# One core: a cached attention block beside an MLP at decode, with x's rows issued by SyncE between wq's two blocks and the last but one piece of w2b in three parts

## The chip, the core and the metric

The kernel runs on one core of a Trainium2 chip. The metric is the device time of one execution in microseconds; the figure given is the median of several runs. A core has five engines that run their own instruction streams and meet at semaphores: TensorE (PE, matmuls), VectorE (DVE), ScalarE (ACT), GpSimd (POOL) and SyncE (SP). DMA transfers are issued from an engine's stream, go into a queue, and are carried by the core's 16 DMA engines.

## The reference

For two tokens (B = 2, one position each) of width 1024 it computes, in fp32:

```python
xn = layernorm(x)
q = (xn @ wq).reshape(2, 1, 32, 128)            # 32 query heads, 4 key/value heads
scores = q · k_cache * 128 ** -0.5              # 32768 cached positions
o = softmax(scores) · v_cache
out = x + o.reshape(2, 1, 4096) @ wo + silu(xn @ w1) @ w2    # w1: 1024 x 3584, w2: 3584 x 1024
```

The caches and weights are 331 MB, each element of which is used once. The term `x` in the last line is the residual.

## The kernel before

All large inputs pass through two SBUF buffers, `bufA` and `bufB`, of 128 partitions x 16384 floats (8 MB each). A fill of a buffer is called a step here; there are 40: wq in two blocks, w1 in two (w1b, then w1a), for each of eight pairs of key/value head and token two blocks of keys (kt) and two of values (v0, v1), wo in two, and w2 in two (w2a in two pieces, w2b in seven). Even steps use bufA and odd ones bufB. The host lays every block out so that a partition's row is contiguous in memory.

SP issues all fills in order, from `load` (L161 to L164). Before it refills a buffer it waits on the semaphore `freed`, which DVE raises when TensorE has ended the step that read the buffer. Fills are thus issued while the fill of the other buffer is still on its way. TensorE waits at the start of a step for the fill's landing (`ld`, and `more` for a second piece) and for its stationary operand (`tok`), then runs 32 matmuls of 128x512 in the profile's form, 64 instructions. TensorE's array is used as four strips of 32 rows of output each, so that x or the weights stand in `weights` as blocks of 32 columns.

**The head.** SP issues wq's first block (L109). POOL clears `xs` (L112) and then `blank` (L113), an area that holds the identity, several small operands, and `xres`. ACT waits for the first memset and issues x8 (L115): eight rows of x into every 16th partition of `xs`. The eight rows are the two tokens, four times each, turned by a quarter of the width each time, so that the first 256 columns of the eight rows together hold all of x. ACT then waits for the second memset and issues x again in four rows into `xres` (L117), for the residual. SP waits for x8's landing (`ldx`, L118) before it issues wq's second block (L119). DVE waits for x8 as well and computes the layernorm (L133 to L147): statistics over all columns, normalisation of the first 256 columns, a 32x32 transpose into `xT`, and copies into `weights` (L153, one by DVE for step 0 and one by POOL for step 1). From there TensorE can start step 0.

After step 0 DVE raises `freed` and ACT copies the result out of PSUM (L184); with `freed` at 1 SP issues w1b, at 2 w1a.

**The tail.** w2b comes in seven pieces with a semaphore each (L177 to L179). The first two (3072 and 1024 KB) belong to the step's ordinary matmuls; the last five are the five arrays `last`: three pieces of 512 KB, one of 384 KB and one of 128 KB. The last two are one tile of w2 (128 rows x 1024 columns), cut at 192 of every 256 columns. Meanwhile POOL adds up the partial results and the residual (L319 to L323), DVE adds the last partial result (L325, L327), and TensorE, after the tiles of the first two of the five pieces (L398, L399), folds that sum into its accumulator `acc` by matmuls with `fold` (L400 to L402), and runs the remaining three tiles (L403 to L405). `tile` waits for its piece (L394). ACT copies `acc` out (L242), SP issues the store of the output (L330) and waits for it.

Of the kernel before, what the change touches and what calls it, by code (L numbers as in the profile page):

```python
# [8 lines left out]
B, HQ, HKV, SK, DH, D, F = 2, 32, 4, 32768, 128, 1024, 3584  # L9
P = 128  # L10
REP = HQ // HKV
W = 16384
NC = SK // W
KT = D // P
FT = F // P
QW = D // 4
CUT = 3 * QW // 4
LOOPS = HKV * B
STEPS = 4 + 4 * LOOPS + 4
# [29 lines left out]
        self.eng.sem_inc(token, -n)  # L49


def gqa_plus_mlp_kernel(nc, x, x8, kt, v0, v1, wq, wo, w1a, w1b, w2a, w2b, out):


    pe, dve, act, pool = (Stream(nc, e, n) for e, n in
                          ((nc.tensor, "pe"), (nc.vector, "dve"), (nc.scalar, "act"), (nc.gpsimd, "pool")))
    sp, T, V, A, G = nc.sync, nc.tensor, nc.vector, nc.scalar, nc.gpsimd
    sems = [pe.sem, dve.sem, act.sem, pool.sem]

    def sem(name):  # L60
        sems.append(nc.alloc_semaphore(name))
        return sems[-1]

    def sb(name, *shape):
        return nc.alloc_sbuf_tensor(name, shape, F32).ap()
# [3 lines left out]

    buf = [sb(n, P, W) for n in ("bufA", "bufB")]  # L70
    ld, more, tok = ([sem(f"{n}{k}") for k in "AB"] for n in ("ld", "more", "tok"))
    ldx, ldr, done, turn_sem, self_sem = (sem(n) for n in ("ldx", "ldr", "done", "marks", "self"))
    freed, subbed, normed, tq, pself = (sem(n) for n in ("freed", "subbed", "normed", "tq", "pself"))
    trm, tgd, tls, tob = (sem(n) for n in ("trm", "tgd", "tls", "tob"))
    last = [sem(f"last{i}") for i in range(5)]
# [3 lines left out]
    xs, xT = sb("xs", P, D), sb("xT", P, KT, 32)  # L79
    stats, mv, ln = sb("stats", P, 2, V.BN_STATS_DIM), sb("mv", P, 2), sb("ln", P, 6)  # L80
    ev = [sb(f"ev{i}", P, 1024) for i in range(4)]
# [2 lines left out]
    pre, sig, rsig = sb("pre", P, FT, 32), sb("sig", P, FT, B), sb("rsig", P, FT, B)  # L84
    onew = sb("onew", P, REP)
    ones = sb("ones", P, P)
    blank, used = sb("blank", P, P + 32 + 160 + 3 * REP + 1024 + 32 * (HQ + FT)), [0]

    def zeroed(*shape):
        n = shape[0] * (shape[1] if len(shape) > 1 else 1)  # L90
        lo = used[0]
        used[0] += n
        t = blank[:, lo:lo + n]
        return t.rearrange("p (a m) -> p a m", m=shape[1]) if len(shape) > 1 else t

    ident, sel, fold, rm, lsum, gd, ob, xres = (zeroed(n) for n in (P, 32, 160, REP, REP, REP, 512, 512))
    oT, hT = zeroed(HQ, 32), zeroed(FT, 32)
    rest, ot = sb("rest", P, 512), sb("ot", P, QW)
    gm, gmax, rl = sb("gm", REP, 1), sb("gmax", P, 1, REP), sb("rl", P, REP)
# [5 lines left out]
    def mm(o, lhsT, rhs, start=True, stop=True):  # L105
# [5 lines left out]

    z_x = pool.mark(G.memset(xs, 0.0))  # L112
    z = pool.mark(G.memset(blank, 0.0))  # L113
    act.wait(z_x)
    A.dma_start(xs[::16, :], x8).then_inc(ldx, 16)  # L115
    act.wait(z)
    A.dma_start(xres[0:64:16, :], x).then_inc(ldr, 16)  # L117
    sp.wait_ge(ldx, 16)  # L118
    sp.dma_start(buf[1], wq[1]).then_inc(ld[1], 16)  # L119

    pool.wait(z)
    t = pool.mark(G.affine_select(out=ident, in_=ident, compare_op=ALU.not_equal, fill=1.0, base=0,
                                  pattern=[[-1, P]], channel_multiplier=1))
    pool.wait(t)
    halves = fold[:, 32:].rearrange("p (a m) -> p a m", m=64)[:, :, :32]
    t = pool.mark(G.tensor_add(halves, *(ident[:, 64 * g:64 * g + 64].rearrange("p (a m) -> p a m", m=32)
                                         for g in range(2))))
# [6 lines left out]
    for i in range(2):  # L134
        t = dve.mark(V.bn_stats(stats[:, i, :], xs[:, i * 512:(i + 1) * 512]))
    dve.wait(t)
    t = dve.mark(V.bn_aggr(mv, stats))
    var, std, y0, t0, t1, rstd = (ln[:, i:i + 1] for i in range(6))
    dve.wait(t)
    t = dve.mark(V.tensor_scalar_add(var, mv[:, 1:2], EPS))  # L140
    act.wait(t)
    t = act.mark(A.activation(std, var, AF.Sqrt))
    for f in (lambda: V.reciprocal(y0, std), lambda: V.tensor_mul(t0, y0, y0), lambda: V.tensor_mul(t1, t0, var),
# [5 lines left out]
        t = dve.mark(f())  # L149
# [11 lines left out]
    def load(k, dst, src, s, n):  # L161
        if n:
            sp.wait_ge(freed, n)
        sp.dma_start(buf[k][:, dst] if isinstance(dst, slice) else dst, src).then_inc(s, 16)  # L164
# [4 lines left out]
    for it in range(LOOPS):  # L169
        h, b = divmod(it, B)  # L170
# [4 lines left out]
    load(0, slice(0, W // 2), w2a[:, :W // 2], ld[0], STEPS - 3)  # L175
    load(0, slice(W // 2, W), w2a[:, W // 2:], more[0], 0)
    cuts = [0, 6 * D, 8 * D, 9 * D, 10 * D, 11 * D, 11 * D + 4 * CUT, 12 * D]  # L177
    for lo, hi, s in zip(cuts, cuts[1:], [ld[1], more[1], *last]):
        load(1, slice(lo, hi), w2b[:, lo:hi], s, STEPS - 2 if lo == 0 else 0)  # L179


    for n in range(4):
        act.wait((freed, n + 1))
        t = act.mark(A.copy(ev[n], ps[n % 2]))  # L184
# [4 lines left out]
        a, b = ev[n][:, :512], ev[n][:, 512:]  # L189
        if n < 2:  # L190
            i_sumq = pool.mark(G.tensor_add(sumq[:, 512 * n:512 * n + 512], a, b))  # L191
        elif n == 2:
            t = pool.mark(G.tensor_add(sumh[:96, 512:], a[:96, :384], b[:96, :384]))
            for j in range(3):
                pool.wait(t)
                t = pool.mark(G.tensor_add(sumh[96:, 512 + P * j:512 + P * (j + 1)], a[32 * j:32 * j + 32, 384:],
                                           b[32 * j:32 * j + 32, 384:]))
# [15 lines left out]
    t = dve.mark(V.transpose(pre.rearrange("p t m -> p (t m)"), sumh))  # L213

    act.wait(t)
    t = act.mark(A.activation(sig, pre[:, :, ::16], AF.Exp, scale=-1.0))
    for f in (lambda: V.tensor_scalar_add(sig, sig, 1.0), lambda: V.reciprocal(rsig, sig),
              lambda: V.tensor_mul(hT[:, :, ::16], pre[:, :, ::16], rsig)):
        dve.wait(t)
        t = dve.mark(f())  # L220
# [8 lines left out]
    for it in range(LOOPS):  # L229
        h, b = divmod(it, B)  # L230
# [86 lines left out]
        G.tensor_copy(wt[c][:, :2 * n].rearrange("p (t d) m -> p t d m", d=2),  # L317
                      hT[:, 16 * c:16 * c + n, None, :].to_broadcast([P, n, 2, 32])).then_inc(tok[c], 1)
    t = pool.mark(G.tensor_add(ev[0], ev[0], ev[1]))  # L319
    pool.wait(t, (ldr, 16))  # L320
    t = pool.mark(G.tensor_add(ev[0][:, :512], ev[0][:, :512], xres))
    pool.wait(t, outs[2])
    t = pool.mark(G.tensor_add(ev[0], ev[0], ev[2]))  # L323
    dve.wait(t)
    t = dve.mark(V.tensor_add(rest, ev[0][:, :512], ev[0][:, 512:]))  # L325
# [64 lines left out]
    def quarter(o, lhsT, w, start=False, stop=False):  # L390
        return [mm(o[32 * j:32 * j + 32, :], lhsT[j], w[j], start, stop) for j in range(4)][-1]

    def tile(t, o, lo, n, start=False, stop=False):
        T.wait_ge(last[t], 16)  # L394
        at = buf[1][:, lo:lo + 4 * n].rearrange("p (j n) -> p j n", j=4)
        return quarter(o, [hT[:, min(24 + t, FT - 1), :]] * 4, [at[:, j] for j in range(4)], start, stop)

    pe.mark(tile(0, acc, 8 * D, QW, True))  # L398
    tile(1, acc, 9 * D, QW)  # L399
    T.wait_ge(tob, 1)  # L400
    for c in range(2):
        mm(acc, fold[:, 32 - 32 * c:160 - 32 * c], ob[:, c * QW:(c + 1) * QW], False, False)  # L402
    tile(2, acc, 10 * D, QW)  # L403
    tile(3, acc[:, :CUT], 11 * D, CUT)
    pe.mark(tile(4, acc[:, CUT:], 11 * D + 4 * CUT, QW - CUT, False, True))  # L405
# [46 lines left out]
```

## Time and profile before

| | |
|---|---|
| median of 3 runs | 773.11 us (773.10 to 773.14) |
| profiled execution | 773.19 us |
| its span, first to last instruction | 771.8 us |
| bytes read from memory | 331.39 MB |
| TensorE matmul busy | 396.3 us (51%) |
| VectorE, ScalarE, GpSimd busy | 132.4, 28.4, 45.4 us |
| mean granted TensorE clock | 0.746 |

The table is read from the bottom up to the bytes: no engine is busy for more than about half of the span, while 331 MB in 771.8 us are 429 GB/s on average. The profile's views speak of instructions by line and engine; SPq and ACTq rows are DMA issues, in which the duration is that of the issuing instruction and not of the transfer. The list of DMA issues gives the time from issue to landing, which includes the time that a transfer spends behind others in the queue. In brackets behind an instruction stands how long its engine was idle before it, and what ended that.

### The profile page before, as it was taken

Reading aid. Unit: us, or ns where it says so; the run is one execution under the profiler, and the core shown is the slowest. Engines: PE = TensorE matmul, PEld = TensorE weight load, DVE = VectorE, ACT = ScalarE, POOL = GpSimd, SP = SyncE. Lnnn points to the kernel's source line nnn. Section 1 sums busy time; section 2 is a strip of 40 time slices with the busy share of each in tenths; the row PEclk is TensorE's granted clock in tenths of the full one; section 3 lists DMA queues with packets and bytes.
Section 4 is the critical chain, followed back from the end, with each engine's and each line's share of the span. In section 5 each row is a group of like instructions: output and inputs, shape, how many; then the busy total and the mean of one; then the engine's idle time right before and its main releaser. Section 6 shows DMA issues by size and latency. Waiting matters only on the chain. (4 is left out here: it accounts for less than half of the span.)

```text
span 771.8 us, 6114 instructions
## 1 busy us (share of the span) xinstructions
PE 396.3 (51%) x2702; PEld 126.3 (16%) x2702; DVE 132.4 (17%) x99; ACT 28.4 (4%) x37; POOL 45.4 (6%) x73
## 2 busy tenths in 40 slices
PE   0545545464546454545454546554545454545566
PEld 0111111121112111211121112111211121112122
DVE  2000103030403030303130403031303130303000
ACT  0000100100010001000100010001000100010000
POOL 3001200001000100010001000100010001000121
PEclk9976766767776667776767776667776777776688
DMA  9999999999999999999999999999999999999997
GB/s 383 435 435 435 435 435 435 435 435 435 435 435 435 435 435 435 435 431 435 435 435 435 435 435 435 435 435 435 428 435 435 431 435 421 425 431 425 431 433 329
DMA packets 6953, 331.43 MB, mean 429 GB/s; under 512 B 780, under 2 KB 924, under 8 KB 1448
## 3 DMA queue, kind: packets, MB, share of 16 engines
q1 hardware_dynamic: 6928, 331.37, 99.4%
q10 hardware_dynamic: 24, 0.04, 0.0%
q8 instruction: 1, 0.02, 0.0%
HBM read 331.39 MB, written 0.02 MB: 429 GB/s over the span
## 5 line engine op out<-in xcount | busy, mean ns | idle before, releaser
L106 PE MATMUL xy<-bufB,weights 128*32 128x512 f32 x1248 | 179.6, 740 | 167.4 <-PEq L49 167.4
L106 PE MATMUL xy<-bufA,weights 128*32 128x512 f32 x1280 | 183.7, 738 | 96.9 <-PEq L49 96.9
L106 PEld LDWEIGHTS xy<-bufB,weights 128*32 128x32 f32 x1248 | 49.4, 133 | 297.8 <-issue 297.7
L106 PEld LDWEIGHTS xy<-bufA,weights 128*32 128x32 f32 x1280 | 50.6, 132 | 213.5 <-issue 213.4
L257 DVE STREAM_TRANSPOSE st<-xy 128x2048 f32<-128x2048 f32 x8 | 18.5, 2317 | 243.2 <-PE xy L106 243.2
L270 DVE TENSOR_REDUCE blank<-xy 128x512 f32<-128x2048 f32 x8 | 18.3, 2292 | 224.5 <-PE xy L106 224.5
L285 POOL MEMSET weights<- 128x1024 f32 x16 | 15.2, 951 | 525.4 <-POOLq L49 525.4
L106 PE MATMUL smA<-blank 128*8 128x128 f32 x20 | 5.4, 371 | 51.9 <-PEq L49 51.9
L106 PE MATMUL smA<-blank,ones 128*128 128x8 f32 x18 | 4.9, 347 | 50.6 <-PEq L49 50.6
L259 DVE TENSOR_REDUCE blank<-st 128x8 f32<-128x2048 f32 x8 | 30.5, 3808 | 0.3
L271 DVE TENSOR_REDUCE blank<-weights 128x8 f32<-128x2048 f32 x8 | 30.4, 3799 | 0.0
L233 ACT ACTIVATE weights<-st 128x1024 f32<-128x1024 f32 x16 | 16.0, 1048 | 328.3 <-DVE st L267 328.3
L267 DVE TENSOR_TENSOR st<-st,gmax 128x2048 f32<-128x2048 f32 x8 | 18.3, 2291 | 0.3
L106 PE MATMUL smB<-blank 128*128 128x8 f32 x72 | 15.9, 350 | 0.0
L106 PEld LDWEIGHTS smB<-blank 128*128 128x128 f32 x72 | 15.6, 318 | 0.0
L106 PEld LDWEIGHTS smA<-blank,ones 128*128 128x128 f32 x18 | 4.3, 298 | 58.5 <-issue 58.5
L236 ACT COPY blank<-onew 128x8 f32<-128x8 f32 x8 | 1.6, 204 | 279.5 <-DVE onew L275 279.5
L106 PEld LDWEIGHTS smA<-blank 128*8 128x8 f32 x20 | 1.3, 88 | 60.2 <-issue 60.2
L325 DVE TENSOR_TENSOR rest<-ev 128x512 f32<-128x512 f32 x1 | 0.7, 691 | 49.2 <-POOL ev L323 49.2
L290 POOL COPY weights<-qall 128x128 f32 x32 | 8.4, 291 | 4.2 <-POOL weights L285 3.1
L106 PE MATMUL smB<-blank,ones 8*128 8x8 f32 x20 | 5.3, 334 | 5.7 <-PEq L49 5.7
L209 DVE STREAM_TRANSPOSE tqs<-sumq 128x1024 f32<-128x1024 f32 x1 | 1.2, 1246 | 39.2 <-POOL sumq L191 39.2
(53 smaller groups left out, 58.2 us busy)
## 6 DMA issues: line engine op xcount, KB each, us to landing
bufA<-in_w2a SPq DMA_DIRECT2D x2, 4096.0 KB, 22.5
bufA<-in_w1b SPq DMA_DIRECT2D x1, 6144.0 KB, 23.7
bufB<-in_w2b SPq DMA_DIRECT2D x1, 3072.0 KB, 17.1
bufB<-in_w2b SPq DMA_DIRECT2D x3, 512.0 KB, 20.8
bufB<-in_w2b SPq DMA_DIRECT2D x1, 1024.0 KB, 19.2
bufB<-in_w2b SPq DMA_DIRECT2D x1, 384.0 KB, 22.1
bufA<-in_kt SPq DMA_DIRECT2D x8, 27.4
bufB<-in_kt SPq DMA_DIRECT2D x8, 29.0
```

The costliest lines, as they stand in the source:

```text
L106: return T.matmul(o, lhsT, rhs, start=start, stop=stop)
L209: i_q = dve.mark(V.transpose(tqs.rearrange("p c m -> p (c m)"), sumq))
L233: A.activation(wt[c].rearrange("p e m -> p (e m)"), st[:, 1024 * c:1024 * c + 1024], AF.Exp, scale=SCALE).then_inc(tok[c], 1)
L236: A.copy(oT[:, REP * h:REP * (h + 1), 16 * b], onew).then_inc(tq, 1)
L257: t = mine(V.transpose(st, xy))
L259: V.tensor_reduce(rm, e8.rearrange("p n m -> p m n"), AX.X, ALU.max).then_inc(trm, 1)
L267: V.tensor_sub(e8, e8, gmax.to_broadcast([P, 256, REP])).then_inc(subbed, 1)
L270: V.tensor_reduce(ob, xy.rearrange("p (c n) -> p n c", c=4), AX.X, ALU.add).then_inc(tob, 1)
L271: V.tensor_reduce(lsum, weights.rearrange("p e (r m) -> p m (e r)", m=REP), AX.X, ALU.add).then_inc(tls, 1)
L285: G.memset(wt[c], 0.0).then_inc(pself, 1)
L290: m = G.tensor_copy(o, q[:, None, None, :].to_broadcast([P, 4, 4, REP]))
L325: t = dve.mark(V.tensor_add(rest, ev[0][:, :512], ev[0][:, 512:]))
```

## The change

x8 is no longer issued by ACT but by SP, between wq's two blocks, after SP has waited for the memset of `xs`. SP does not wait for x8's landing any more. The second transfer of x, its buffer `xres` and its semaphore `ldr` are gone: the quarters of the eight rows are ordered differently, so that columns 256 to 767 of the rows in partitions 0, 16, 32 and 48 hold x as the residual needs it; POOL adds these columns from `xs` (64 partitions instead of 128). The layernorm changes only the first 256 columns. Since the first 256 columns of the rows now come in another order of quarters, the host reorders the rows of wq and w1 to match.

The 384 KB piece of w2b is issued as three transfers, of the rows (partitions) 0 to 63, 64 to 113 and 114 to 127. They share one semaphore, for which the tile waits at 48 instead of 16.

```diff
-    act.wait(z_x)
-    A.dma_start(xs[::16, :], x8).then_inc(ldx, 16)
-    act.wait(z)
-    A.dma_start(xres[0:64:16, :], x).then_inc(ldr, 16)
-    sp.wait_ge(ldx, 16)
+    sp.wait_ge(z_x[0].sem, z_x[1])
+    sp.dma_start(xs[::16, :], x8).then_inc(ldx, 16)
     sp.dma_start(buf[1], wq[1]).then_inc(ld[1], 16)
...
-    for lo, hi, s in zip(cuts, cuts[1:], [ld[1], more[1], *last]):
-        load(1, slice(lo, hi), w2b[:, lo:hi], s, STEPS - 2 if lo == 0 else 0)
+    for i, s in enumerate([ld[1], more[1], *last]):
+        rows = [0, 64, 114, P] if s is last[3] else [0, P]
+        for a, b in zip(rows, rows[1:]):
+            load(1, buf[1][a:b, cuts[i]:cuts[i + 1]], w2b[a:b, cuts[i]:cuts[i + 1]], s, 0 if i else STEPS - 2)
...
-    pool.wait(t, (ldr, 16))
-    t = pool.mark(G.tensor_add(ev[0][:, :512], ev[0][:, :512], xres))
+    pool.wait(t)
+    t = pool.mark(G.tensor_add(ev[0][:64, :512], ev[0][:64, :512], xs[:64, 256:768]))
...
-        T.wait_ge(last[t], 16)
+        T.wait_ge(last[t], 48 if t == 3 else 16)
...
-    w1 = np.asarray(B_w1)
+    wq, w1 = (np.asarray(a).reshape(4, QW, -1)[[2, 0, 1, 3]].reshape(D, -1) for a in (A_wq, B_w1))
...
-        "x": np.ascontiguousarray(xr.reshape(B, 2, 512).transpose(1, 0, 2)).reshape(4, 512),
-        "x8": np.stack([np.roll(xr, -QW * g, axis=1) for g in range(4)]).reshape(8, D),
+        "x8": np.stack([xr.reshape(B, 4, QW)[:, o] for o in ((2, 0, 1, 3), (0, 2, 3, 1), (1, 0, 2, 3), (3, 0, 1, 2))]
+                       ).reshape(8, D),
```

The start of SP's stream before (each row: the line, the operation, its output and input by name, and the output's shape; `in_wq` is wq in memory, `in_w1b` and `in_w1a` are w1):

```order
L109 DMA bufA<-in_wq 128x16384
L119 DMA bufB<-in_wq 128x16384
L164 DMA bufA<-in_w1b 128x2x6144
L164 DMA bufB<-in_w1a 128x16384
L164 DMA bufA<-in_kt 128x16384
```

And after:

```order
L109 DMA bufA<-in_wq 128x16384
L115 DMA xs<-in_x 8x1024
L116 DMA bufB<-in_wq 128x16384
L161 DMA bufA<-in_w1b 128x2x6144
L161 DMA bufB<-in_w1a 128x16384
```

x's eight rows have moved into SP's stream ahead of wq's second block, which waited for them before; everything behind keeps its order.

On ACT, where the two transfers of x stood ahead of the table load and the square root of the layernorm, the difference is:

```order
-L115 DMA xs<-in_x 8x1024
-L117 DMA blank<-in_x 4x512
-L142 ACT_TABLE_LOAD
-L142 ACTIVATE ln<-ln 128x1
+L139 ACT_TABLE_LOAD
+L139 ACTIVATE ln<-ln 128x1
 L184 COPY ev<-xy 128x1024 x4
```

The two transfers are gone, and with them the two waits for POOL's memsets; the table load is ACT's first instruction now.

The end of SP's stream before (`in_w2a` and `in_w2b` are w2; the rows of 1024, 768 and 256 columns are the five pieces of the tail):

```order
L164 DMA bufA<-in_w2a 128x8192 x2
L164 DMA bufB<-in_w2b 128x6144
L164 DMA bufB<-in_w2b 128x2048
L164 DMA bufB<-in_w2b 128x1024 x3
L164 DMA bufB<-in_w2b 128x768
L164 DMA bufB<-in_w2b 128x256
L330 DMA out_y<-ot 16x256
```

And after:

```order
L161 DMA bufB<-in_w2b 128x1024 x3
L161 DMA bufB<-in_w2b 64x768
L161 DMA bufB<-in_w2b 50x768
L161 DMA bufB<-in_w2b 14x768
L161 DMA bufB<-in_w2b 128x256
L330 DMA out_y<-ot 16x256
```

The row of 128 partitions x 768 columns has become three, at the same place; the last piece and the store stand behind them as before.

More of the change, by code (lines that the diff above doesn't have):

```diff
@@ L49, in take, with gqa_plus_mlp_kernel @@
         self.eng.sem_inc(token, -n)
-def gqa_plus_mlp_kernel(nc, x, x8, kt, v0, v1, wq, wo, w1a, w1b, w2a, w2b, out):
+def gqa_plus_mlp_kernel(nc, x8, kt, v0, v1, wq, wo, w1a, w1b, w2a, w2b, out):
     pe, dve, act, pool = (Stream(nc, e, n) for e, n in
@@ L71, in gqa_plus_mlp_kernel @@
     ld, more, tok = ([sem(f"{n}{k}") for k in "AB"] for n in ("ld", "more", "tok"))
-    ldx, ldr, done, turn_sem, self_sem = (sem(n) for n in ("ldx", "ldr", "done", "marks", "self"))
+    ldx, done, turn_sem, self_sem = (sem(n) for n in ("ldx", "done", "marks", "self"))
     freed, subbed, normed, tq, pself = (sem(n) for n in ("freed", "subbed", "normed", "tq", "pself"))
@@ L86, in gqa_plus_mlp_kernel @@
     ones = sb("ones", P, P)
-    blank, used = sb("blank", P, P + 32 + 160 + 3 * REP + 1024 + 32 * (HQ + FT)), [0]
+    blank, used = sb("blank", P, P + 32 + 160 + 3 * REP + 512 + 32 * (HQ + FT)), [0]
     def zeroed(*shape):
@@ L94, in zeroed @@
         return t.rearrange("p (a m) -> p a m", m=shape[1]) if len(shape) > 1 else t
-    ident, sel, fold, rm, lsum, gd, ob, xres = (zeroed(n) for n in (P, 32, 160, REP, REP, REP, 512, 512))
+    ident, sel, fold, rm, lsum, gd, ob = (zeroed(n) for n in (P, 32, 160, REP, REP, REP, 512))
     oT, hT = zeroed(HQ, 32), zeroed(FT, 32)
@@ L434 @@
         "v1": lay(v[:, :, 1], (B, HKV, 2, 4, 4, 4, 4, 32, DH), (0, 1, 4, 7, 2, 5, 6, 3, 8), (B, HKV, P, W)),
-        "wq": np.stack([lay(A_wq, qd, (4, 0, 3, 1, 6, 2, 5, 7), (2, P, W))[0],
-                        lay(A_wq, qd, (4, 0, 3, 1, 2, 6, 5, 7), (2, P, W))[1]]),
+        "wq": np.stack([lay(wq, qd, (4, 0, 3, 1, 6, 2, 5, 7), (2, P, W))[0],
+                        lay(wq, qd, (4, 0, 3, 1, 2, 6, 5, 7), (2, P, W))[1]]),
         "wo": np.stack([lay(A_wo, split, (0, 4, 1, 3, 5, 2, 6), (2, P, W))[0],
```

## The prediction

> **What bounds the kernel now.** I read the page's throughput rows first, then the issues with their time to landing, then the head and the tail as timelines.
>
> ```profile
> GB/s 383 435 435 435 435 435 435 435 435 435 435 435 435 435 435 435 435 431 435 435 435 435 435 435 435 435 435 435 428 435 435 431 435 421 425 431 425 431 433 329
> HBM read 331.39 MB, written 0.02 MB: 429 GB/s over the span
> q10 hardware_dynamic: 24, 0.04, 0.0%
> q8 instruction: 1, 0.02, 0.0%
> ```
>
> Between a low first and a low last slice the rate stands at about 435 GB/s; the engines never set it. The next rows say whether the queue of loads ever runs dry (SP's issues in order of time, then KB of each and us to landing, from the list of issues).
>
> ```profile
> 0.74 0.37 SPq L109 DMA_DIRECT2D bufA<-in_wq  x1
> 10.77 0.33 SPq L119 DMA_DIRECT2D bufB<-in_wq  x1
> 33.85 0.67 SPq L164 DMA_DIRECT2D bufA<-in_w1b  x1
> 52.07 0.34 SPq L164 DMA_DIRECT2D bufB<-in_w1a  x1
> ...
> bufA<-in_w1b SPq DMA_DIRECT2D x1, 6144.0 KB, 23.7
> ...
> bufA<-in_wq SPq DMA_DIRECT2D x1, 22.9
> ...
> bufB<-in_wq SPq DMA_DIRECT2D x1, 32.2
> bufB<-in_w1a SPq DMA_DIRECT2D x1, 24.8
> ...
> out_y<-ot SPq DMA_DIRECT2D x1, 16.0 KB, 1.8
> ```
>
> Issue plus time to landing: wq's first block lands at 23.64, the second at 42.97, w1b at 57.55, w1a at 76.87. The steps are 19.33 us for 8.39 MB (434 GB/s), 14.58 us for 6.29 MB (431 GB/s), 19.32 us for 8.39 MB: no gap, although the second block was issued only at 10.77. The tail, with the issue of each last piece and its time to landing:
>
> ```profile
> 746.26 0.91 SPq L164 DMA_DIRECT2D bufB<-in_w2b  x2
> 746.73 0.91 SPq L164 DMA_DIRECT2D bufB<-in_w2b  x2
> ...
> bufB<-in_w2b SPq DMA_DIRECT2D x1, 512.0 KB, 21.6
> bufB<-in_w2b SPq DMA_DIRECT2D x1, 384.0 KB, 22.1
> bufB<-in_w2b SPq DMA_DIRECT2D x1, 128.0 KB, 21.9
> ...
> 766.16 0.69 DVE L327 TENSOR_TENSOR blank<-rest,xy 128x512 f32<-128x512 f32 x1 [1.00 <-PE acc L106]
> ...
> 767.23 0.73 PEld L106 LDWEIGHTS acc<-blank 128*128 128x128 f32 x4 [0.41 <-DVE blank L327]
> ...
> 768.29 0.16 PEld L106 LDWEIGHTS acc<-bufB,blank 128*32 128x32 f32 x8 [0.33 <-issue]
> 768.29 0.64 PE L106 MATMUL acc<-bufB,blank 128*32 128x256 f32 x8
> 768.53 0.72 PE L106 MATMUL acc<-bufB,blank 128*32 128x256 f32 x8
> 768.88 0.16 PEld L106 LDWEIGHTS acc<-bufB,blank 128*32 128x32 f32 x8 [0.43 <-DMA bufB<-in_w2b]
> 769.59 0.37 ACT L242 COPY ot<-acc 128x256 f32<-128x256 f32 x1 [7.68 <-PE acc L106]
> 769.99 0.55 SPq L330 DMA_DIRECT2D out_y<-ot  x1
> ```
>
> Issues stand some 0.47 us apart, so the 384 KB piece (at 746.73) lands at 768.83 and the 128 KB piece (at 747.20) at 769.10. From 23.64 to 769.10, 323.0 MB arrive in 745.5 us: 433 GB/s. So the time is the first landing, that stream, and 2.7 us behind it. An edit moves the time only if it lets the queue run dry, or moves the last landings and what follows them.
>
> **The head.** SP's wait for x goes, and with it ACT's two small transfers; x8 now stands in SP's own queue behind wq's first block.
>
> ```profile
> SPq L119 <- DMA xs<-in_x: 9.6, 1, 9.6
> ...
> 1.62 2.84 POOL L113 MEMSET blank<- 128x3288 f32 x1
> 1.72 1.15 ACTq L115 DMA_DIRECT2D xs<-in_x  x1
> 10.78 1.29 DVE L135 BATCH_NORM_STATS2 stats<-xs 128x6 f32<-128x512 f32 x2 [10.78 <-DMA xs<-in_x]
> 14.66 0.69 DVE L153 COPY weights<-xT 128x1024 f32<-128x1024 f32 x1
> 23.88 9.86 PE L106 MATMUL xy<-bufA,weights 128*32 128x512 f32 x64 [23.88 <-PEq L49]
> 25.56 0.23 PEld L106 LDWEIGHTS xy<-bufA,weights 128*32 128x32 f32 x4 [0.63 <-issue]
> 26.41 0.23 PEld L106 LDWEIGHTS xy<-bufA,weights 128*32 128x32 f32 x4 [0.63 <-issue]
> ```
>
> The 9.6 us that SP waited is no gain: wq's second block was queued by 11.1 and not needed before 23. What the wait's removal costs is x: it came at 10.78, amid the first block; now its rows stand behind that block. The pieces of w2b, issued back to back on this queue, land in order of issue, so I put x's landing between 22.8 (just behind most of wq's first block) and 23.85 (0.2 behind its landing). From x's landing to the end of DVE's spread copy takes 15.35 - 10.78 = 4.57 us: layernorm, transpose, copy. TensorE, which waited for wq (landed 23.64, started 23.88), now waits for that copy: it starts between 27.5 and 28.5, I take 28.0, about 4.1 us later. With 9.86 us for the first step, and 0.11 from 33.74 to SP's issue at 33.85, w1b is issued near 38.0 instead of 33.85.
>
> Does the queue run dry? It is full until wq's second block has landed, at 42.97. The nearest row for issue to landing of an almost empty transfer is out_y's 1.8 us, so an issue by 42.97 - 1.8 = 41.2 leaves no gap. The margin is 3.2 us. The cost is 0, and if the margin is overrun each microsecond costs one. From the other side: had TensorE the slow pitch throughout (0.85 us per four weight loads, 16 such groups, 13.7 us) and the latest start, w1b would be issued at 42.3 and the queue be dry for 1.1 us. After that nothing is late: the second step waits for wq's second block at 42.97 as before, and w1a's 24.8 us to landing, against 19.3 for its bytes, hold another 5 us.
>
> The small parts. The 8 KB that gave the residual go: 0.02 us at 435 GB/s. The blank memset shrinks by 512 of 3288 columns (0.44 of 2.84 us on POOL, which then idles until x's transpose). SP's wait for the memset of xs (over when the next memset starts, at 1.62) costs nothing: SP's first issue ended at 1.11, and the next block is needed at 23. ACT's table load, behind its DMAs until now, comes earlier and has 20 us. POOL's residual add waited for nothing late:
>
> ```profile
> 748.57 1.26 POOL L321 TENSOR_TENSOR ev<-ev,blank 128x512 f32<-128x512 f32 x1
> 762.06 2.38 POOL L323 TENSOR_TENSOR ev<-ev 128x1024 f32<-128x1024 f32 x1 [12.23 <-ACT ev L240]
> ```
>
> On 64 partitions it takes at most the same 1.26 us, and 12.23 us of idle time follow: cost 0.
>
> **The tail.** Two more issues on SP, 0.47 us each, put the last one near 748.1, 20 us ahead of its data: 0. What changes is which DMA engines carry the 128 rows of 3 KB. The split of 50 and 14 rows is not in this trace. Spread evenly over 16 engines it would change nothing. The other bound comes from q10: its 24 packets for eight and four rows are a packet and a count for each row, so as many engines as rows. If rows go to engines in equal whole numbers (64 as 16 x 4, 50 as 10 x 5, 14 as 14 x 1), ten engines carry 10 rows instead of 8, the others 4 or 5. An engine moves 433/16 = 27.1 GB/s, a row takes 0.11 us, so the ten end 0.23 us later and the rest 0.34 to 0.45 earlier. Which one ends last the views don't tell; the one 16 KB program fetch (q8), if one engine carries it, keeps that engine 16 KB / 27.1 GB/s = 0.6 us behind to the end, since the queue never idles. If that engine is lightened, the piece lands earlier, but TensorE can't use much: the eight matmuls of w2b's tile before go in two groups 0.24 us apart (768.29, 768.53), so the next could have started at 768.77 instead of 768.88, a gain of 0.11. If it is burdened, the loss is 0.23. I take the middle, nothing.
>
> [...]
>
> **The sum** against the profiled execution: span 771.8, 1.39 us around it, 773.19. Head 0, bytes -0.02, tail 0: 773.2. It ran 0.08 above the median of the runs, so 773.1 in terms of the median.
>
> **The rivals.**
> *Half of SBUF at a time.* 64 rows fill partitions 0 to 63, the other two pieces 64 to 127. If a transfer to half of the partitions goes at half the rate, the piece takes longer. It took 768.83 - 767.86 = 0.97 us (the 512 KB piece before it landed at 746.26 + 21.6); the three in a row at half rate would take 1.94, and less where engines that are done go on to the 128 KB piece. Price +0.4 to +0.9, less the 0.11 that TensorE has: 773.7. It decides once the 384 KB land over 0.1 us later. The trace has no load of half the partitions to speak for or against.
> [...]
> *x comes with the second block (slower).* If x's rows land only with wq's second block, at 42.97, TensorE starts at 47.6, w1b is issued at 57.6, and the queue is dry for 57.6 - 41.2 = 16 us: 789. It decides from an x landing at 23.85 + 2.8 = 26.6. Against it: the landings in order of issue. For it: x needed 9 us on its own queue for 32 KB.
> *Few engines for 50 rows (slower).* On one engine 50 rows of 3 KB take 50 x 0.113 = 5.7 us, less what it would have carried (0.9): 778. 0.2% is reached from some 14 rows more than the present 8 on the engine that ends last.
> *A shorter tail (faster).* At most the 0.43 us before the tile's weights go, if the folds also come earlier: 772.7. Only a head or a stream quicker by 1.5 us would be faster by 0.2%; no row shows anything to gain there.
>
> **How the numbers follow.** 0.2% is 1.55 us, about what a measurement of this kernel can tell from no change. Forecast 0.62 (772.8 to 773.4); half of SBUF 0.23 (773.5 to 774.0); shorter tail 0.08 (772.5 to 772.8); x with the second block 0.03; few engines 0.03; something unseen in the stream 0.01. The range 772.6 to 774.0 leaves out about 0.1. Slower by over 0.2%: 0.06; faster: 0.01; within: 0.93.
>
> **What would show it.** Right: q10 gone; wq's second block issued near 2.2 and landing still near 43; TensorE's first matmul near 28 and w1b issued near 38, landing still near 57.5; three issues of 192, 150 and 42 KB; the weights of the next to last tile between 768.8 and 769.1. Wrong: w1b landing later than 58.5 (the head ran dry); that tile waiting beyond 769.3 (half ports), or beyond 770 (few engines); x landing after 27.

## The result and the profile after

The changed kernel took 774.21 us, the median of 22 runs (773.70 to 775.96), against 773.25 us for the kernel before in 22 runs (772.92 to 773.91). The medians are 0.96 us apart; the ratio on record is 1.0014, with a 95% interval of 1.0007 to 1.0020. That is inside the 0.2% called "no change", but clear of zero and 0.2 us above the upper end of the predicted range. Of those 0.2 us, 0.14 are the reference: the prediction counted from 773.11, the median of the first three runs.

The profiled execution has a span of 773.1 us (before: 771.8). First the head, from the list of SP's issues, the list of issues with KB and time to landing, and the timeline of the kernel after:

```profile
1.71 0.73 SPq L115 DMA_DIRECT2D xs<-in_x  x1
2.48 0.39 SPq L116 DMA_DIRECT2D bufB<-in_wq  x1
37.54 0.62 SPq L161 DMA_DIRECT2D bufA<-in_w1b  x1
...
bufA<-in_w1b SPq DMA_DIRECT2D x1, 6144.0 KB, 20.2
...
bufA<-in_wq SPq DMA_DIRECT2D x1, 23.1
bufB<-in_wq SPq DMA_DIRECT2D x1, 40.7
...
22.93 1.29 DVE L132 BATCH_NORM_STATS2 stats<-xs 128x6 f32<-128x512 f32 x2 [22.93 <-DMA xs<-in_x]
...
27.66 9.76 PE L106 MATMUL xy<-bufA,weights 128*32 128x512 f32 x64 [27.66 <-PEq L49]
```

x lands at 22.93, 12 us later than before; TensorE starts at 27.66 instead of 23.88, and w1b is issued at 37.54 instead of 33.85. wq's second block lands at 2.48 + 40.7 = 43.18 and w1b at 37.54 + 20.2 = 57.74: 14.56 us for 6.29 MB, as before (14.58). The queue did not run dry.

The tail of the kernel before, as far as it was not shown yet: the issue of the second 512 KB piece (this row takes in the third's) and the median time to landing of the three such pieces, which is the second's:

```profile
745.78 0.91 SPq L164 DMA_DIRECT2D bufB<-in_w2b  x2
...
bufB<-in_w2b SPq DMA_DIRECT2D x3, 512.0 KB, 20.8
```

The tail of the kernel after, first the issue and the time to landing of the second and the third 512 KB piece, then rows of the timeline:

```profile
745.99 0.43 SPq L161 DMA_DIRECT2D bufB<-in_w2b  x1
...
bufB<-in_w2b SPq DMA_DIRECT2D x1, 512.0 KB, 21.0
...
746.47 0.43 SPq L161 DMA_DIRECT2D bufB<-in_w2b  x1
...
bufB<-in_w2b SPq DMA_DIRECT2D x1, 512.0 KB, 22.8
...
767.55 0.73 PEld L106 LDWEIGHTS acc<-blank 128*128 128x128 f32 x4 [0.41 <-DVE blank L327]
...
769.32 0.16 PEld L106 LDWEIGHTS acc<-bufB,blank 128*32 128x32 f32 x8 [1.04 <-DMA bufB<-in_w2b]
...
770.14 0.48 PEld L106 LDWEIGHTS acc<-bufB,blank 128*32 128x32 f32 x16 [0.66 <-DMA bufB<-in_w2b]
...
770.85 0.37 ACT L242 COPY ot<-acc 128x256 f32<-128x256 f32 x1 [8.72 <-PE acc L106]
```

Here is the loss. The third 512 KB piece lands at 746.47 + 22.8 = 769.27, 2.28 us behind the second (745.99 + 21.0 = 766.99); before, the two stood 1.28 us apart (745.78 + 20.8 = 766.58 and 767.86). This piece was not touched by the change: it is only ahead of the cut one in the queue. Its tile, which before started at 768.29 with nothing to wait for, now waits 1.04 us for its data, and the next another 0.66. From the weights of the folds to ACT's last copy it takes 770.85 - 767.55 = 3.30 us, against 769.59 - 767.23 = 2.36 before: 0.94 of the 1.26 us by which that copy is later. The other 0.32 us stand ahead of the folds (wq's first block landed at 23.84 instead of 23.64, and the rest gathers on the way to the tail); the runs below show that such 0.3 us come and go between kernels with the same head (with the head of the kernel after, the folds' weights come at 767.05 in one profile and at 767.36 in another).

### The profile page after: what moved, and what is told of

The parts are those of the page before. It is cut to its first block, busy times and chain, and to the rows that moved or that the text cites. A ratio compares the mean times of both kernels' runs of the same rounds, so it can differ in the third digit from the quotient of the medians.

```text
span 773.1 us, 6114 instructions
## 1 busy us (share of the span) xinstructions
PE 395.6 (51%) x2702; PEld 125.9 (16%) x2702; DVE 132.4 (17%) x99; ACT 28.4 (4%) x37; POOL 44.9 (6%) x73
## 3 DMA queue, kind: packets, MB, share of 16 engines
q1 hardware_dynamic: 6968, 331.40, 99.4%
## 6 DMA issues: line engine op xcount, KB each, us to landing
bufA<-in_w1b SPq DMA_DIRECT2D x1, 6144.0 KB, 20.2
bufB<-in_w2b SPq DMA_DIRECT2D x1, 1024.0 KB, 19.3
```

## The experiments

Three causes were to be told apart in the tail: that each of the three row groups fills only half of SBUF's partitions (half of SBUF), that 50 and 14 rows load the 16 DMA engines unevenly (uneven engines), and that three transfers cost more than one. A fourth, the late x, would cost in the head.

In each result the time behind "against" is that of the kernel before in the same series, and in brackets stands the 95% interval of the ratio. "Folds to copy" is the time from the weights of the folds to ACT's last copy in the profile: 2.36 us before, 3.30 after.

**The head alone.** The kernel after, with the 384 KB piece in one transfer again.

```diff
-        rows = [0, 64, 114, P] if s is last[3] else [0, P]
+        rows = [0, P]
...
-        T.wait_ge(last[t], 48 if t == 3 else 16)
+        T.wait_ge(last[t], 16)
```

> The head of the change alone: x issued by SP between wq's blocks, residual from xs, but the 384 KB piece of w2b in one transfer. If the loss of 0.96 us lies in the tail (half of SBUF at a time, or uneven engines), this stands within 0.3 us of before, 773.1 to 773.5, and the 384 KB piece lands about 0.97 us after the one ahead of it. If the late x costs it (the queue running dry in the head), it shows most of the 0.96 us: about 774.1.

Measured: 773.33 us against 773.16, ratio 1.0002 (0.9992 to 1.0011). No loss that can be told from none; from the folds to ACT's copy it takes 769.44 - 767.05 = 2.39 us. The medians are 0.17 us apart, well inside the interval.

**The tail alone.** The kernel before, with the piece as 64, 50 and 14 rows.

```diff
-    for lo, hi, s in zip(cuts, cuts[1:], [ld[1], more[1], *last]):
-        load(1, slice(lo, hi), w2b[:, lo:hi], s, STEPS - 2 if lo == 0 else 0)
+    for i, s in enumerate([ld[1], more[1], *last]):
+        rows = [0, 64, 114, P] if s is last[3] else [0, P]
+        for a, b in zip(rows, rows[1:]):
+            load(1, buf[1][a:b, cuts[i]:cuts[i + 1]], w2b[a:b, cuts[i]:cuts[i + 1]], s, 0 if i else STEPS - 2)
```

> The tail of the change alone: 64, 50 and 14 rows, with x still issued by ACT. Every theory that puts the loss in the tail expects 773.9 to 774.3; the theory of the head expects 773.2 to 773.3, as before.

Measured: 774.31 us against 773.16, ratio 1.0017 (1.0008 to 1.0026); folds to copy 3.19 us. The tail alone has a loss as large as that of the whole change. Its timeline divides it otherwise than that of the kernel after:

```profile
768.22 0.16 PEld L106 LDWEIGHTS acc<-bufB,blank 128*32 128x32 f32 x8 [0.55 <-DMA bufB<-in_w2b]
...
769.40 0.48 PEld L106 LDWEIGHTS acc<-bufB,blank 128*32 128x32 f32 x16 [1.03 <-DMA bufB<-in_w2b]
```

Here the tile of the third 512 KB piece waits 0.55 us, and that of the cut piece 1.03.

**The same three sizes, cut by columns.** The kernel before, with 192, 150 and 42 KB of all 128 rows each.

```diff
+        wide = cuts[i + 1] - cuts[i]
         for a, b in zip(rows, rows[1:]):
-            load(1, buf[1][a:b, cuts[i]:cuts[i + 1]], w2b[a:b, cuts[i]:cuts[i + 1]], s, 0 if i else STEPS - 2)
+            lo, hi = cuts[i] + wide * a // P, cuts[i] + wide * b // P
+            load(1, buf[1][:, lo:hi], w2b[:, lo:hi], s, 0 if i else STEPS - 2)
```

> Before, with the 384 KB piece in three transfers of the same sizes (192, 150 and 42 KB), cut by columns: each has all 128 rows, so all of SBUF's partitions and the same load on each engine. Half of SBUF at a time, and uneven engines, both expect no loss: 773.1 to 773.4. If three issues, three landings and a wait for 48 are what costs, it shows +0.7 to +1.0: about 774.1.

Measured: 773.40 us against 773.16, ratio 1.0003 (0.9994 to 1.0012); folds to copy 770.14 - 767.59 = 2.55 us. Three issues, three landings and the wait for 48 are not the cause: the medians are 0.24 us apart, inside the interval.

**64, 48 and 16 rows.** The tail alone once more, with `rows = [0, 64, 112, P]`: by the author's estimate every one of the 16 engines carries eight rows (4 + 3 + 1), as before the change.

> Before, with the 384 KB piece as 64, 48 and 16 rows: each number a multiple of 16, so each of 16 engines carries 4 + 3 + 1 = 8 rows as before, but the first piece still fills partitions 0 to 63 alone and the others 64 to 127. Half of SBUF at a time expects most of the loss: +0.6 to +1.0, 773.9 to 774.2, with the 512 KB piece ahead landing late too. Uneven engines expect 773.2, as before.

Measured: 774.40 us against 773.16, ratio 1.0016 (1.0007 to 1.0025), 0.2 us above the expected range. Its tail in the timeline:

```profile
767.29 0.73 PEld L106 LDWEIGHTS acc<-blank 128*128 128x128 f32 x4 [0.41 <-DVE blank L329]
...
769.28 0.16 PEld L106 LDWEIGHTS acc<-bufB,blank 128*32 128x32 f32 x8 [1.26 <-DMA bufB<-in_w2b]
...
770.13 0.48 PEld L106 LDWEIGHTS acc<-bufB,blank 128*32 128x32 f32 x16 [0.69 <-DMA bufB<-in_w2b]
...
770.84 0.37 ACT L244 COPY ot<-acc 128x256 f32<-128x256 f32 x1 [10.00 <-PE acc L106]
```

Folds to copy 3.55 us, and the same wait for the untouched 512 KB piece. With the rows split evenly the loss stays, so the uneven split is not needed for it. That the split was even is read from packets. Besides the views, the packed trace holds every increment of a semaphore: 780 in the kernel before and 800 in the kernel after, without those at the issues, and as many packets are under 512 B. A transfer of 128 rows has sixteen of either, and x's eight rows have eight. They are taken here as one for each engine that carried the transfer; no trace names the engine. The head alone has 6944 packets in its main queue and the kernel after 6968, which is 16 + 10 + 14 - 16 more; this kernel has 6960 and the kernel before 6928, which is 3 x 16 - 16 more.

```profile
q1 hardware_dynamic: 6968, 331.40, 99.4%
...
q1 hardware_dynamic: 6944, 331.40, 99.4%
...
q1 hardware_dynamic: 6960, 331.37, 99.4%
...
q1 hardware_dynamic: 6928, 331.37, 99.4%
```

**The disputed cost by itself.** The kernel before, with wq's first block in two halves, by partitions and, as control, by columns. TensorE waits for the added semaphore before its first step.

```diff
-    sp.dma_start(buf[0], wq[0]).then_inc(ld[0], 16)
+    sp.dma_start(buf[0][:64], wq[0][:64]).then_inc(first, 16)
+    sp.dma_start(buf[0][64:], wq[0][64:]).then_inc(ld[0], 16)
...
-    sp.dma_start(buf[0], wq[0]).then_inc(ld[0], 16)
+    sp.dma_start(buf[0][:, :W // 2], wq[0][:, :W // 2]).then_inc(first, 16)
+    sp.dma_start(buf[0][:, W // 2:], wq[0][:, W // 2:]).then_inc(ld[0], 16)
```

> The disputed cost by itself, on a large transfer: before, with wq's first block (8.39 MB) issued as partitions 0 to 63 and then 64 to 127. Half of SBUF at half the rate expects twice 9.7 us for each half, so wq's first landing near 43 instead of 23.6 and a time of 790 to 792.5 (some less where engines drift apart into different halves). If the number of transfers or something else in the tail were the cause, it is 773.2 and the landing 23.6.

> The control to the former: before, with wq's first block issued as its first and its last 8192 columns, 128 partitions each. Every theory expects 773.1 to 773.5 and a landing near 23.7; a loss of more than 1 us would make the cut itself the cause.

Measured, one run each: 794.21 us by partitions and 773.18 by columns, against 773.21. The first is 1.7 us above its expected range. Of the kernel cut by partitions, two stretches of the view by windows (start and end, length, the busy time and instructions of the five rows of engines, granted clock, DMA share, GB/s), and TensorE's first matmul; last, a stretch of the kernel cut by columns:

```profile
5.00:20.00 15.00, 0.00 (x0) 0.00 (x0) 1.05 (x2) 1.28 (x1) 0.72 (x4) 1.00 1.03 212
20.00:40.00 20.00, 0.00 (x0) 0.00 (x0) 2.94 (x11) 0.20 (x1) 1.56 (x1) 1.00 1.02 210
...
45.15 9.85 PE L107 MATMUL xy<-bufA,weights 128*32 128x512 f32 x64 [45.15 <-PEq L49]
...
2.00:40.00 38.00, 9.82 (x64) 2.67 (x64) 4.00 (x12) 2.50 (x3) 6.29 (x7) 0.95 1.01 432
```

The rate is 210 to 212 GB/s, 0.49 of the 434 that a block on all partitions gets, with the DMA engines busy all along; cut by columns it is 432. The halves land at 24.5 and 44.9, and TensorE starts at 45.15 instead of 23.88. The price is 21.0 us, somewhat more than the 19.3 of exactly half the rate. All 16 engines take part in either half: the DMA share of 1.02 to 1.03 is a mean over 16 engines, and the kernel has 6944 packets in its main queue, 16 more than before. One thing these runs do not separate: a half by partitions is also one connected half of the block in memory, and a half by columns is not.

**x behind both blocks.** The head alone, with the two lines of x and of wq's second block exchanged.

> The head of the change with x issued behind both blocks of wq instead of between them. By the reckoning of the head, x lands near 42.2, TensorE starts near 47, w1b is issued near 57 and the queue is dry for about 16 us: 788 to 790. If the head had cover that the reckoning does not see (TensorE not needed for w1b so early), the time stays within 3 us of before.

Measured, one run: 790.42 us against 773.21, just above the expected range. TensorE's first step, the view by windows, and the time to landing of w1b:

```profile
46.79 9.94 PE L106 MATMUL xy<-bufA,weights 128*32 128x512 f32 x64 [46.79 <-PEq L49]
...
40.00:45.00 5.00, 0.00 (x0) 0.00 (x0) 2.45 (x9) 0.20 (x1) 0.00 (x0) 1.00 0.02 7
45.00:50.00 5.00, 3.21 (x16) 0.91 (x20) 1.55 (x3) 0.00 (x0) 1.56 (x1) 1.00 0.00 0
50.00:57.00 7.00, 7.00 (x60) 2.07 (x56) 0.00 (x0) 0.15 (x1) 0.00 (x0) 1.00 0.00 0
...
bufA<-in_w1b SPq DMA_DIRECT2D x1, 6144.0 KB, 17.9
```

The queue is empty from wq's second landing, at 42.7, until w1b is issued at 56.84. w1b lands at 74.74 instead of 57.55, and these 17.2 us go whole into the time. So the reckoning of the head holds on its other side too: x between the blocks is covered, x behind them is not.

**The change with its tail put right.** The kernel after, with the three transfers cut by columns as above.

> The whole change with one thing put right: the three transfers of the 384 KB piece are cut by columns instead of rows, so that each fills all 128 partitions. If the loss is the half of SBUF alone, it goes: 773.2 to 773.5, as head_only (773.33) and tail_columns (773.40). If something arises only where the new head and a cut tail meet, 774 or more.

Measured: 773.41 us against 773.23, ratio 1.0002 (0.9993 to 1.0012); folds to copy 769.90 - 767.36 = 2.54 us. Without the cut by rows the loss is gone: what is left, 0.18 us by the medians, can't be told from nothing.

**TensorE's code without the far jump.** The kernel before, with the block `te_far` standing where TensorE's stream begins.

```diff
-    T.br("te_far")
+    T.reg_mov(pair, 0)
+    T.reg_mov(half, 0)
+    pe.wait(i_const)
+    for s, n in ((trm, 1), (tgd, 1), (tls, 1), (tob, 1), (more[0], 16 * PAIRS - 16), (more[1], 16 * PAIRS - 16)):
+        T.sem_inc(s, n)
+    T.br("te_loop")
```

> Before, with TensorE's first block of code (registers and semaphores set) standing where its stream begins instead of at its end, so that it does not jump there and back. Theory: the one 16 KB program fetch at about 1.9 us holds one DMA engine back, every landing in the tail waits for that engine, and the jump causes the fetch; then the fetch goes, and the time falls by 0.4 to 0.8 us to 772.4 to 772.8. If the fetch belongs to another stream, it stays, and the time is 773.1 to 773.3.

Measured: 773.72 us against 773.21, ratio 1.0006 (0.9997 to 1.0015): no gain, if anything a loss, and outside both expected ranges. The fetch did not go, it moved. Of this kernel, the issues of the head, and the queue row of the stretch from 48.0 to 50.5 us, in which the 16 KB packet now lies (before, it lies between 1 and 4 us):

```profile
bufA<-in_w1b SPq DMA_DIRECT2D x1, 6144.0 KB, 25.0
...
bufA<-in_wq SPq DMA_DIRECT2D x1, 22.0
...
10.61 0.33 SPq L119 DMA_DIRECT2D bufB<-in_wq  x1
32.99 0.68 SPq L164 DMA_DIRECT2D bufA<-in_w1b  x1
...
bufB<-in_wq SPq DMA_DIRECT2D x1, 31.5
...
q8 instruction: 1, 0.02, 2.7%
```

wq's first block lands at 22.74 instead of 23.64, 0.9 us earlier; but from wq's second block (42.11) to w1b (57.99), the stretch with the fetch, it takes 15.88 us instead of 14.58, 1.3 us more. The lag stays: w1b lands 0.44 us later than before, and the folds of the tail come 0.44 us later (767.67 against 767.23).

The increments show more. In this kernel the sixteen of wq's second block come between 41.84 and 42.15. At the next transfer, w1b, fifteen have come by 56.72 and the last comes at 58.01, and at the third 512 KB piece of the tail it is still 1.2 us behind (767.12 and 768.33). In the kernel before, where the fetch starts at 1.89, the last is 0.6 us behind the other fifteen from wq's first block (22.96 and 23.59) to the last piece of w2b (768.59 and 769.14). Read as engines, one of them falls behind where the fetch falls, and stays behind.

The one packet of 16 KB came at 48.70 instead of 1.89 when the early jump was taken out. That a jump asks for it was the author's theory; what asked for it at 48.70 is not shown.

**Less work for some engines.** The kernel before, with the last 320 columns of wq's first block issued as 110 and 18 rows.

```diff
-    sp.dma_start(buf[0], wq[0]).then_inc(ld[0], 16)
+    SIDE = 320
+    sp.dma_start(buf[0][:, :W - SIDE], wq[0][:, :W - SIDE]).then_inc(ld[0], 16)
+    for a, b in ((0, 110), (110, P)):
+        sp.dma_start(buf[0][a:b, W - SIDE:], wq[0][a:b, W - SIDE:]).then_inc(first, 16)
```

> Before, with the last 320 columns of wq's first block issued as 110 and 18 rows, which by whole divisors go to ten and nine DMA engines: six engines then carry 10 KB less and nine 6 KB more. If one of those six is the engine that the program fetch holds back, and every landing of the tail waits for it, each microsecond it gains is one gained until the others are last: 772.8 to 773.0, about 0.3 below before. If the held back engine is one of the others, or the tail does not wait for it, 773.2 to 773.5. The runs scatter by 0.3, so it may stay unclear; the landing times in the trace then decide.

Measured: 774.00 us against 773.23, ratio 1.0008 (0.9999 to 1.0017): no gain, and above both expected ranges. wq's second block (issued at 10.51) lands 33.2 us later, at 43.71 instead of 42.97, and all that follows is as late.

```profile
q1 hardware_dynamic: 7076, 331.37, 99.4%
```

How the rows go to the engines was the author's estimate, and it had one count wrong. These are 148 packets more than before: 110 + 11 + 18 + 9. Read as engines, the 110 rows went to eleven of ten rows each, not to ten, and five engines were relieved, not six. The increments of wq's second block show the rest: five come between 42.11 and 42.27, ten between 42.78 and 42.95, and the last at 43.74. The one that is behind was thus not among the five, but still 0.8 us behind the ten. Why the ten came some 0.6 us later than before, where the reckoning had 0.2, stays open. No version that beats the kernel before by more than the scatter was found.

## Why the prediction was wrong

**The head: right.** x was put between 22.8 and 23.85 and came at 22.93; TensorE's start at 28.0 and came at 27.66; w1b's issue at 38.0 and came at 37.54, with landing near 57.5 (57.74). The cost of 0 is borne out by the head alone (ratio 1.0002, interval 0.9992 to 1.0011), and its price without cover, put at 789, nearly by x behind both blocks (790.42). One term was too small there: the 1.8 us of out_y as the time ahead at which an issue leaves no gap. On the empty queue w1b took 17.9 us to land, 3.3 more than the 14.58 that it takes in the stream. The margin was thus about 1.7 us and not 3.2; it was still not used up. The small parts (POOL's memset and residual add, ACT's table load, the 8 KB) are inside that nothing.

**The tail: the step that failed** is "I take the middle, nothing". It weighed only which engines carry how many rows, at -0.11 to +0.23 us. The split that it assumed fits the counts: the packets add up with 16 + 10 + 14 (6968 against 6944), and the semaphore of the cut piece has as many increments, 40, between 767.60 and 770.09, behind two early ones at the issues. But with an even split the loss is there all the same (64, 48 and 16 rows: 1.0016), and with the split by columns it is not (1.0003). What costs is the cut by rows, each group on at most half of the partitions. The rival "half of SBUF at a time" was the right one, and it stood with a chance of 0.23 where the forecast had 0.62; a row for it was missing in the trace before, and it was taken as a doubt beside the sum. The last line of the prediction calls it "half ports"; no run shows ports, and what the runs showed is the rate by partitions, 210 to 212 GB/s, against 432 by columns.

**The rival's size was short as well**: 773.7 against 774.21. It priced the 384 KB piece alone, at most 0.97 us longer, less 0.11. It left out the piece ahead: the third piece landed 2.28 us behind the second instead of 1.28. The increments of these two pieces show how. At each, one of the sixteen comes behind the other fifteen; with the cut by rows it falls back further at the third piece (us; in brackets by how much the last is behind):

| | second piece: fifteenth, last | third piece: fifteenth, last |
|---|---|---|
| before | 766.02, 766.62 (0.60) | 767.31, 767.90 (0.59) |
| the change with its tail cut by columns | 766.14, 766.74 (0.60) | 767.43, 768.05 (0.62) |
| after | 766.05, 766.94 (0.89) | 767.77, 769.28 (1.51) |
| 64, 48 and 16 rows | 765.95, 766.68 (0.73) | 767.81, 769.24 (1.43) |
| the tail alone | 765.92, 766.32 (0.40) | 767.52, 768.17 (0.65) |

The account that fits is this: while fifteen engines already write the rows of the cut piece to half of the partitions, the last is still writing its share of the third piece, and is slowed. It is argued from these times; the increments name neither engine nor partition. Where the last is 0.7 to 0.9 us behind to begin with, most of the loss stands at the third piece: from the folds to that piece's tile it takes 0.71 us more than before in the profile after, of 0.94 in all, and 0.93 of 1.19 with 64, 48 and 16 rows. Where it is 0.4 us behind, in the profile of the tail alone, it is 0.23 of 0.83, and most of the loss stands at the cut piece.

**The other rivals.** Few engines for the 50 rows: the packets add up with ten for them, so it does not apply. The prediction's own sign would have misled here: the next to last tile came at 770.14, beyond the 770 that was set for few engines, and it is the counts and not the time that rule this rival out. x with the second block: x came before wq's first landing. A shorter tail: the tile before the cut one waited longer instead.

Why half of the partitions take bytes at half the rate is not shown: the runs show 210 to 212 GB/s by partitions and 432 by columns, and do not exclude that the half of the block in memory has a part in it.

## What to carry to other kernels

Try a cut by columns before one by rows: halves of the partitions issued one after the other each kept all 16 DMA engines busy here (a share of 1.02 to 1.03) and yet ran at half the rate (210 to 212 GB/s, against 432 by columns), and with a cut by rows the whole transfer ahead in the queue landed later too (2.28 us behind the one ahead of it instead of 1.28). Where a stream of loads sets the time, ask of each edit whether the queue runs dry, which can be reckoned from issues and landings, and then whether it changes the rate at which bytes arrive. The time ahead at which the next transfer has to be issued is better taken from a large transfer on an empty queue (3.3 us here, of w1b's 17.9) than from a small one (1.8, the store of the output). A small load that others wait for could stand behind a large one here (x 12 us later, ratio 1.0002 for the head alone), since what it delayed, w1b's issue at 37.54, was needed only when the next large one had landed, at 43.18.

## What was not expected

The 16 KB packet of the queue of kind `instruction`, taken here as a fetch of program code. It is one packet among 6953, and one of a transfer's sixteen increments comes behind the other fifteen from then on: by 0.6 us in the kernel before, by 1.2 to 1.3 us where the fetch fell at 48.70. A wait for all of a transfer ends with that one (the last for wq's first block came at 23.59, and TensorE started at 23.88). The lag lasts as long as the queue does not empty: with x behind both blocks, where it is empty for 14 us, the last increment is 0.7 us behind the others ahead of the pause (42.00 and 42.69) and 0.07 us behind it (74.71 and 74.78). By the estimate of 27.1 GB/s for one engine (433 / 16), 16 KB are worth 0.6 us; why the lag was twice that at 48.70 is open. wq's first landing lies between 23.3 and 23.8 us in the profiles of the other kernels with the same first transfer, and such tenths pass through to the end: the scatter of the runs of the kernel before, mostly some 0.3 us to either side, is of this size, though that the fetch makes all of it was not shown.

x landed ahead of the large block that it stood behind: its use was released at 22.93, wq's landing was at 23.84. The increments say why: the eight for x's eight rows come between 22.43 and 22.91, and fifteen of wq's have come by 22.97; only the last, at 23.81, is late. x's eight rows did not wait for that last one.
